# Turning k, q and y on VectorE in squares of 32, with y taken through DRAM

## The chip, the cores and the metric

One core of a Trainium2 chip. The metric is the device time of one execution in microseconds (us), the median of several executions. Executions of a kernel on one core mostly lie within 1%; each comparison below was made on one chip, in rounds that ran the two kernels alternately. An execution more than 1.5% above the fastest of its kernel is called slow; comparisons use the others.

Names: PE is TensorE (matmul), DVE is VectorE, ACT is ScalarE, POOL is GpSimd, SP is SyncE, which here issues nearly all DMAs. A line number such as L90 is that of the kernel's text; the changed kernel's numbers are shifted. The granted clock is the share of its full clock that PE was given; in these traces it is at any moment either 1 or 0.5.

## The reference

```python
q, k, v, o_gate: (4, 8, 768, 40)      # batch, heads, sequence, head dim; gates (4, 8, 768)
for t in range(S):                    # mLSTM: a decayed sum of v k^T, read with q
    C = f * C + i * outer(v[t], k[t]);  n = f * n + i * k[t]
    y[t] = sigmoid(o_gate[t]) * (C @ q[t]) / max(|n . q[t]|, 1)
x = y.transpose(0, 2, 1, 3).reshape(3072, 320)
out = ((x @ w1) * (x @ w2)) @ w3 @ w_out      # float64 weights, d_ff = 1024
```

## The kernel before

The sequence is cut into 24 units: 6 pieces of 128 tokens times 4 batches. The main loop has one step per unit and then some more. In step s, PE turns k and q of unit s (tiles pt), turns y of unit s - 3 (px), runs a product of w3 and w_out (wp, steps 10 to 17) or two output tiles (po, from step 17; step 17 has both), then the up-projections of an older group (pa, pb) and last the "cell": outputs of unit s - 1, state and scores of unit s.

```python
def turn(n):                                   # k and q, [token, head dim] -> [head dim, token]
    for src, dst, name in ((kbuf[n % NB], kT_t, "kT"), (qbuf[n % NBQ], qT_t, "qT")):
        pt = mps([128, NP, P], "pt")
        for p in range(NP):
            transpose(pt[:, p, :], src[:, 2 * p:2 * p + 2, :].rearrange("p a b -> p (a b)"))   # PE
        dst[n] = sb.tile([128, NP, P], FP, name=name, tag=name)
        nc.scalar.copy(out=dst[n], in_=pt)                                                    # ACT

def x_trans(n):                                # y -> xT, the input of the up-projections
    ...
    px = mps([128, KF + 1, P], "px")
    for cc in range(KF + 1):
        transpose(px[:, cc, :], y[:, cc * P:(cc + 1) * P])                                    # PE
    nc.scalar.copy(out=x_t[gr][:, :, j * P:(j + 1) * P], in_=px)                              # ACT
```

The weights are float64 words. DVE makes floats of them, one piece of 128 rows by 512 at a time: five operations on 128x512 and, for w3, a transpose. Up to step 15 there are one to three such conversions per step (`n_cvt`), two in each of steps 9 to 15. Before a conversion, ACT scales the raw piece.

```python
def to_f32(dst, raw):                          # L170 to L174
    V.tensor_scalar(out=t, in0=hi, scalar1=3, scalar2=None, op0=OP.logical_shift_left)
    ...                                        # three more
    V.tensor_tensor(out=dst, in0=t.bitcast(FP), in1=r.bitcast(FP), op=OP.add)

for s in range(len(n_up)):                     # the main loop, cut
    if s < NU:
        ...
        if s: turn(s)
    while turned < min(s - 2, NU):
        x_trans(turned); turned += 1
    fold()                                     # wp
    for _ in range(n_down[s]): ffn_out(*downs.pop(0))          # po
    open_ups = [up(*x) for x in now]           # pa, pb
    if len(now) < 2 and turned == s - 2 < NU:
        x_trans(turned); turned += 1
    quarter_work(s, rest)                      # ab, cell, pw, outputs
    ...
    for _ in range(n_cvt[s] if s < len(n_cvt) else 0): convert()
```

PE's instructions are pinned to the order of the program. Those of the other engines are not (after step 6): the compiler's scheduler orders each engine's instructions by its own model of readiness, and on the chip each engine runs its list in that order.

## Time and profile before

| | before |
|---|---|
| median (range) | 493.78 us (493.66 to 494.1) |
| span of the profiled run, granted clock of PE | 494.0 us, 0.98 |
| PE / DVE / ACT busy | 94% / 50% / 31% |
| stage to 146 us | PE with gaps, DVE 60 to over 90% busy |
| stage from 146 us on | PE full; a step is 16.8 us, from step 18 on 21.1 us (step 17, with wp and po, 25.4) |

"DVE 50%" is the mean of a first half in which DVE is nearly full and a second in which it is nearly idle. The slices and the step by step reading are shown in the prediction. One more line, from the view of groups of instructions by form; the columns are line, engine, operation, output and input, count, then busy us and mean ns:

```profile
L223 DVE STREAM_TRANSPOSE w3T<-w 128x512 f32<-128x512 f32 x16 | 11.3, 709 | 0.5
```

DVE's transpose of 128x512 floats took 709 ns here.

### The profile page before, as it was taken

What the parts mean: (1) busy time and instruction counts of PE and PEld (TensorE: products, weight loads), DVE (VectorE), ACT (ScalarE), POOL (GpSimd) and SP (SyncE); (2) the same over time, 40 slices, a digit from 0 to 9 for tenths busy, and PEclk for the clock granted to TensorE, in tenths of its full rate; (3) what the DMA queues carried; (4) which work ended last, traced back from release to release, by engine and by line L of the source; (5) the groups of instructions that cost most, each with busy time, mean ns of one, the idle gap of its engine ahead of it and who ended that gap; (6) DMA issues with size and microseconds to landing.
All of it is one profiled execution on the core that took longest, in us unless ns stands there. A gap on an engine that the chain in (4) does not pass through costs nothing.

```text
span 494.0 us, 13423 instructions
## 1 busy us (share of the span) xinstructions
PE 462.7 (94%) x5714; PEld 380.6 (77%) x5714; DVE 247.5 (50%) x512; ACT 153.5 (31%) x413; POOL 88.6 (18%) x163
## 2 busy tenths in 40 slices
PE   3869797899899999999999999999999998999997
PEld 2759796898677888788878787777878777777864
DVE  7787688999877978977431331403214042111110
ACT  3743454533431543354331322412112011011011
POOL 5431223621311322212410211201000000000000
PEclk9989998989999999999999999999999999999999
DMA  9999936799877737543340422311000000000001
GB/s 186 169 196 197 155 91 130 124 184 180 156 147 136 156 113 152 103 74 56 53 88 15 102 50 56 65 40 41 15 28 1 27 16 15 27 15 13 1 15 40
DMA packets 115404, 42.33 MB, mean 86 GB/s; under 512 B 103120, under 2 KB 106384, under 8 KB 115344
## 3 DMA queue, kind: packets, MB, share of 16 engines
q1 hardware_dynamic: 115200, 41.37, 41.9%
q8 instruction: 45, 0.74, 0.7%
q14 instruction: 15, 0.12, 0.1%
q10 hardware_dynamic: 144, 0.10, 0.1%
HBM read 37.42 MB, written 4.03 MB: 84 GB/s over the span
## 4 chain that ended last, share of the span: by engine, by line
PE 75%; DVE 9%; issue 7%; DMA 3%; SPq 2%; POOL 2%; ACT 1%; DVEq 0%; POOLq 0%; ACTq 0%
PE po L90 21%; PE pa L90 20%; PE pb L90 14%; PE cell L90 7%; PE wp L90 7%; PE pt L93 3%; SPq L154 2%; DVE h L349 1%; DMA raw<-in_moe_w_dram 1%; DMA pw<-U_d 1%; PE px L93 1%; DMA kbuf<-in_k_dram 1%; PE ub L90 1%; DVE h L345 1%; DVE ma L173 1%
## 5 line engine op out<-in xcount | busy, mean ns | idle before, releaser
L514 DVE TENSOR_TENSOR ab<-pb,a_sb 128x512 f32<-128x512 f32 x48 | 33.0, 690 | 182.0 <-ACT a_sb L513 181.9
L90 PE MATMUL po<-w3o,ab 128*128 128x320 f32 x384 | 105.4, 433 | 1.3 <-DVE h L349 1.3
L90 PEld LDWEIGHTS po<-w3o,ab 128*128 128x128 f32 x384 | 72.2, 190 | 30.7 <-issue 1.5
L90 PE MATMUL pa<-xT,w 128*128 128x256 f32 (+1 forms) x448 | 93.0, 355 | 0.0
L90 PE MATMUL pb<-xT,w 128*128 128x256 f32 (+1 forms) x448 | 91.9, 351 | 0.4 <-issue 0.4
L90 PEld LDWEIGHTS pa<-xT,w 128*128 128x128 f32 x448 | 77.1, 195 | 10.7 <-ACT a_sb L513 0.8
L90 PEld LDWEIGHTS pb<-xT,w 128*128 128x128 f32 x448 | 76.3, 192 | 9.0 <-issue 0.6
L513 ACT ACTIVATE a_sb<-pa 128x512 f32<-128x512 f32 x48 | 28.6, 596 | 146.6 <-PE pb L90 146.6
L90 PE MATMUL pb<-xT,wr 64*64 64x256 f32 (+1 forms) x448 | 47.4, 351 | 0.0
L90 PE MATMUL pa<-xT,wr 64*64 64x256 f32 (+1 forms) x448 | 47.4, 351 | 0.0
L283 POOL TENSOR_TENSOR state<-state,decay 128x164 f32<-128x164 f32 x40 | 19.6, 493 | 154.2 <-PE cell L90 99.1
L264 POOL TENSOR_SCALAR_AFFINE_SELECT pw<-pw 64x512 f32<-64x512 f32 x48 | 36.9, 769 | 47.1 <-ACT pw L262 44.6
L262 ACT ACTIVATE pw<-pw,aT 128x64 f32<-128x64 f32 x160 | 40.6, 339 | 5.3 <-DMA pw<-U_d 5.3
L90 PEld LDWEIGHTS pa<-xT,wr 64*64 64x64 f32 x448 | 28.5, 133 | 14.9 <-issue 6.6
L90 PE MATMUL wp<-wo,w3T 128*128 128x320 f32 x128 | 35.9, 433 | 2.0 <-DVE w3T L223 2.0
L521 ACT COPY o_sb<-po 128x320 f32<-128x320 f32 x24 | 10.2, 426 | 74.8 <-PE po L90 74.7
L90 PEld LDWEIGHTS wp<-wo,w3T 128*128 128x128 f32 x128 | 23.7, 190 | 11.1 <-issue 2.2
L90 PEld LDWEIGHTS cell<-vbuf,pw 64*64 64x64 f32 x768 | 28.2, 145 | 2.8 <-issue 0.3
L90 PEld LDWEIGHTS pb<-xT,wr 64*64 64x64 f32 x448 | 28.5, 133 | 0.0
L90 PE MATMUL cell<-vbuf,pw 64*64 64x41 f32 x768 | 28.4, 235 | 0.0
L365 POOL COPY y<-y 128x64 f32<-128x64 f32 x24 | 7.3, 306 | 110.0 <-DVE y L361 109.8
L324 DVE TENSOR_TENSOR pw<-cell,pw 128x512 f32<-128x512 f32 x24 | 16.4, 685 | 19.0 <-PE cell L90 15.4
(89 smaller groups left out, 524.4 us busy)
## 6 DMA issues: line engine op xcount, KB each, us to landing
raw<-in_moe_w_dram SPq DMA_DIRECT2D x64, 128.0 KB, 3.5
pw<-U_d SPq DMA_DIRECT2D x40, 128.0 KB, 3.7
kbuf<-in_k_dram SPq DMA_DIRECT2D x24, 160.0 KB, 4.6
qbuf<-in_q_dram SPq DMA_DIRECT2D x24, 160.0 KB, 4.9
vbuf<-in_v_dram SPq DMA_DIRECT2D x24, 160.0 KB, 4.9
o_in<-in_o_gate_dram SPq DMA_DIRECT2D x24, 160.0 KB, 4.1
out_dram<-o_sb SPq DMA_DIRECT2D x24, 160.0 KB, 1.8
raw<-in_moe_w_dram SPq DMA_DIRECT2D x7, 512.0 KB, 5.8
```

What stands on the lines that cost most here:

```text
L90: in_order(nc.tensor.matmul(out, lhsT=lhsT, rhs=rhs, start=start, stop=stop))
L93: in_order(nc.tensor.transpose(out, in_, ident[0:n, 0:n]))
L154: nc.sync.dma_start(out=dst, in_=src)
L173: V.scalar_tensor_tensor(out=r.bitcast(FP), in0=lo, scalar=2.0 ** -52, in1=r.bitcast(FP), op0=OP.mult, op1=OP.mult)
L262: nc.scalar.activation(out=pw[:, h, :], in_=src[:, h, :], func=AF.Exp, bias=aT[:, c, b * H + h:b * H + h + 1])
L264: nc.gpsimd.affine_select(out=pw[r], in_=pw[r], compare_op=OP.is_ge, fill=0.0, base=0, pattern=[[0, H], [1, L]], channel_multiplier=-1)
L283: nc.gpsimd.tensor_tensor(out=new, in0=old, op=OP.mult, in1=decay[:, b * NP:(b + 1) * NP, 2 * c + x:2 * c + x + 1] .to_broadcast([P, NP, D1]))
L324: first_read = nc.vector.tensor_tensor(out=pv, in0=ss, in1=pv, op=OP.mult)
L365: nc.gpsimd.tensor_copy(out=y_t[n][:, DM:DM + REM], in_=y_t[n][:, KF * P:DM])
L513: nc.scalar.mul(out=a_sb, in_=pa, mul=UP ** -2)
L514: nc.vector.tensor_tensor(out=ab_t[gr][j][:, fs[0]:fs[-1] + 1, t0:t0 + a_sb.shape[-1]], in0=pb, in1=a_sb, op=OP.mult)
L521: nc.scalar.copy(out=o_sb, in_=po)
```

## The change

The intent: take transposes away from PE, the bound, and give them to DVE, which is half idle. DVE's transpose is used here in squares of 32x32 (the prediction says why), so the data must come to it with the squares already in their places. k and q from unit 12 on (the 13th) are loaded from DRAM in such an order (`load_turned`, into what was the gates' space), k a second time, q only so. y from unit 8 on (the 9th) is written to DRAM in pieces (`send`) and read back rearranged (`get_back`). Separately, the first y's transposes on PE are put behind the cell of the third unit, where before they stood ahead of it and PE waited for them. Two smaller edits are cut from the diff below: the cell's matmuls that read kT and qT sum over 40 rows in place of 64, which changed nothing in the length of a full cell (2.50 us in step 11 before and 2.49 after), and the output tile has two buffers in place of three.

```diff
+    N_DVE = 12
+    NY = 8
+    def load_turned(n):                       # 8 DMAs: k and q, four neighbouring tokens to each of 32 partitions
+        ...
     def turn(n):
+        if n >= N_DVE:
+            for src, dst, name in zip(turned_in, (kT_t, qT_t), ("kT", "qT")):
+                dst[n] = sb.tile([128, NP, P], FP, name=name, tag=name)
+                nc.vector.transpose(out=dst[n].rearrange("i p (r f) -> i p f r", f=4),
+                                    in_=src[:, 32:TB].rearrange("i (p f d) -> i p f d", p=NP, f=4)[:, :, :, 0:32])
+            return
+    def send(n): ...                          # 4 DMAs, y -> y_d[n]
+    def get_back(n):
+        back_t[n] = sb.tile([P, 4, KC, 32], FP, name="yb", tag="yb", bufs=1)
+        ...                                   # 4 DMAs, y_d[n] -> yb
+    def x_turn(n):
+        nc.vector.transpose(out=x_t[gr][:, :, j * P:(j + 1) * P].rearrange("c k (m r) -> c k m r", r=32),
+                            in_=back_t.pop(n).rearrange("r m k c -> r k m c"))
...
+        if N_DVE <= s + 1 < NU:
+            load_turned(s + 1)
+        if NY <= s - 3 < NU:
+            get_back(s - 3)
+        if NY <= s - 2 < NU:
+            send(s - 2)
         while turned < min(s - 2, NU):
-            x_trans(turned)
+            x_trans(turned) if turned < NY else x_turn(turned)
...
-        if len(now) < 2 and turned == s - 2 < NU:
+        if len(now) == 1 and turned == s - 2 < NU:
```

More of the change, by code (lines that the diff above doesn't have):

```diff
@@ L95 @@
     halves = [slice(0, L), slice(L, P)]
+    heads = [slice(0, D), slice(DP, DP + D)]
     quarters = ((0, 0), (1, 1), (0, 1), (1, 0))
     NB, NBQ = 4, 3
+    N_DVE = 12
     qbuf = [const.tile([P, H, DP], FP, name=f"qbuf{i}") for i in range(NBQ)]
@@ L109 @@
     U_d = dram.tile([NT, BH, L], FP, name="U_d")
+    NY = 8
+    KC = KF + 1
+    y_d = [dram.tile([P, 4, KC, 32], FP, name=f"y_d{n}") if n >= NY else None for n in range(NU)]
     o_t, u_t = {}, {}
@@ L118, in load @@
         for dst, src in ((kbuf[n % NB][:, :, 0:D], k), (qbuf[n % NBQ][:, :, 0:D], q), (vbuf[n % NB][:, :, 0:D], v)):
-            nc.sync.dma_start(out=dst, in_=rows(src, n))
+            if src is not q or n < N_DVE:
+                nc.sync.dma_start(out=dst, in_=rows(src, n))
+    def load_turned(n):
+        c, b = divmod(n, B)
+        for dst, src in zip(turned_in, (k, q)):
+            for hip in range(2):
+                of = src[b].rearrange("(p two) s d -> two p s d", two=2)[hip, :, c * P:(c + 1) * P, :]
+                for j in range(2):
+                    p0, c0 = hip * DP + j * 32, (1 - j) * 32
+                    nc.sync.dma_start(out=dst[p0:p0 + 32, c0:c0 + NP * RAW].rearrange("r (p e) -> r p e", p=NP),
+                                      in_=of.rearrange("p (r f) d -> r p (f d)", f=4))
     def load_o(n):
@@ L305, in quarter_work @@
                 for hip, x in quarters:
-                    mm(pi[halves[x], hip, p, :], qT[halves[hip], p, halves[x]], before[x][halves[hip], p, :])
+                    mm(pi[halves[x], hip, p, :], qT[heads[hip], p, halves[x]], before[x][heads[hip], p, :])
         n, first_read = s, None
@@ L321, in quarter_work @@
                 for hip, x in quarters:
-                    mm(ss[halves[x], hip, p, :], kT[halves[hip], p, halves[x]], qT[halves[hip], p, halves[x]])
+                    mm(ss[halves[x], hip, p, :], kT[heads[hip], p, halves[x]], qT[heads[hip], p, halves[x]])
             pv = pw.rearrange("p (n two) t -> p two n t", two=2)
@@ L362, in outputs, with send @@
                                 op=OP.mult)
+    def send(n):
+        y = y_t.pop(n)
+        for cc in range(KF):
+            nc.sync.dma_start(out=y_d[n][:, :, cc, :], in_=y[:, cc * P:(cc + 1) * P].rearrange("t (i c) -> t i c", c=32))
+        for i in range(0, 4, 2):
+            nc.sync.dma_start(out=y_d[n][:, i:i + 2, KF, :], in_=y[:, KF * P:DM].rearrange("t (i c) -> t i c", c=32))
+    back_t = {}
+    def get_back(n):
+        back_t[n] = sb.tile([P, 4, KC, 32], FP, name="yb", tag="yb", bufs=1)
+        for i in range(4):
+            nc.sync.dma_start(out=back_t[n][32 * i:32 * (i + 1)].rearrange("r m k c -> r m (k c)"),
+                              in_=y_d[n][:, i].rearrange("(m r) k c -> r m (k c)", r=32))
+    def x_turn(n):
+        gr, j = divmod(n, GT)
+        if j == 0:
+            x_t[gr] = ffn.tile([128, KC, TG], FP, name="xT", tag="xT")
+        nc.vector.transpose(out=x_t[gr][:, :, j * P:(j + 1) * P].rearrange("c k (m r) -> c k m r", r=32),
+                            in_=back_t.pop(n).rearrange("r m k c -> r k m c"))
     def twice(n):
@@ L380 @@
     RG = GR * BH
-    f_sb, a, F, U, on = (const.tile([RG, TC], FP, name=n) for n in ("f_sb", "a", "F", "U", "on"))
+    RAW = 4 * D
+    TB = 32 + NP * RAW
+    gates = const.tile([P, 2 * TB], FP, name="gates")
+    f_sb, a, F, U, on = (gates[0:RG, i * TC:(i + 1) * TC] for i in range(5))
+    turned_in = [gates[:, i * TB:(i + 1) * TB] for i in range(2)]
     w, g = f_sb, on
@@ L416 @@
         nc.gpsimd.memset(t[0], 0.0)
+    nc.gpsimd.memset(gates[:, 5 * TC:2 * TB], 0.0)
+    nc.gpsimd.memset(gates[RG:P, NP * RAW:TB], 0.0)
     nc.gpsimd.memset(pick, 0.0)
@@ L519, in ffn_out @@
             mm(po, ab_t[gr][j // 2][:, f, j % 2 * P:(j % 2 + 1) * P], w3o[:, f, :], start=(f == 0), stop=(f == FO - 1))
-        o_sb = ffn.tile([P, DM], FP, name="o_sb", tag="o_sb", bufs=3)
+        o_sb = ffn.tile([P, DM], FP, name="o_sb", tag="o_sb", bufs=2)
         nc.scalar.copy(out=o_sb, in_=po)
@@ L553 @@
                 turn(s)
-        if 0 <= s - 2 < NU:
+        if N_DVE <= s + 1 < NU:
[4 more added lines that the diff above has]
+            send(s - 2)
+        elif 0 <= s - 2 < NY:
             twice(s - 2)
         while turned < min(s - 2, NU):
-            x_trans(turned)
+            x_trans(turned) if turned < NY else x_turn(turned)
             turned += 1
```

## The prediction

> **What bounds the kernel now.** I read the page first (busy shares and slices), then the chain of waits that ends last, then the timelines of VectorE (DVE) and of the DMA queue (SP). A "step" is one pass of the main loop; step s works on unit s.
>
> The slices, 12.35 us each:
>
> ```profile
> PE   3869797899899999999999999999999998999997
> DVE  7787688999877978977431331403214042111110
> PEclk9989998989999999999999999999999999999999
> ```
>
> PE is full from slice 11 on (about 146 us); before that it has gaps while DVE stands at 7 to 9 tenths. From 160 to 250 us DVE is nearly full too. The chain agrees: from 146 us to the end it is almost pure PE. Step 12 in it (start, duration):
>
> ```profile
> 162.99 1.02 PE pt L93 x8
> 164.01 0.33 PE px L93 x3
> 164.34 4.31 PE wp L90 x16
> 168.65 1.73 PE pa L90 x8
> ...
> 177.44 2.32 PE cell L90 x123
> 179.76 1.02 PE pt L93 x8
> ```
>
> So a step of this stage is pt 1.02 + px 0.33 + wp 4.31 + four pa/pb of 1.73 + 1.89 of remainder + cell 2.32 = 16.78 us, back to back. From step 17 on po (8.62) stands where wp stood: 21.08 us. Everything that leaves PE here leaves the end time, if nothing else takes its place. What DVE does in step 13:
>
> ```profile
> 180.89 0.65 DVE L324 TENSOR_TENSOR pw<-cell,pw 128x512 f32<-128x512 f32 x1
> ...
> 186.55 0.42 DVE L170 TENSOR_SCALAR ex<-raw 128x512 uint32<-128x512 uint32 x1
> ...
> 190.28 0.39 DVE L170 TENSOR_SCALAR ex<-raw 128x512 uint32<-128x512 uint32 x1
> ...
> 194.03 0.69 DVE L514 TENSOR_TENSOR ab<-pb,a_sb 128x512 f32<-128x512 f32 x1 [0.72 <-ACT a_sb L513]
> ...
> 196.61 0.69 DVE L324 TENSOR_TENSOR pw<-cell,pw 128x512 f32<-128x512 f32 x1 [0.69 <-PE cell L90]
> ```
>
> Between two pw lines (one step) DVE waits only 1.38 us for GpSimd, 0.72 and 0.69: it is nearly a second bound. It already starts pw at 180.89, 1.13 us after the cell ended at 179.76. The outputs after pw take about 4.9 us without that long GpSimd wait (165.62 to 170.49 one step earlier), one conversion of a weight piece 190.28 - 186.55 = 3.73 us, and there are two per step up to step 15.
>
> The early stage matters for the last part of the change. The timeline of PE there, and the windows of granted clock (us; busy and count of PE, PEld, DVE, ACT, POOL; clock; DMA share; GB/s):
>
> ```profile
> 33.80 0.88 PE L93 MATMUL px<-ident,y 128*128 128x128 f32 x3 [4.06 <-DVE y L361]
> ```
>
> ```profile
> 36.00:38.00 2.00, 2.00 (x78) 2.00 (x78) 0.63 (x1) 0.00 (x0) 0.00 (x0) 0.50 0.95 297
> ```
>
> PE waits 4.06 us for the first y, and afterwards the clock is half.
>
> **What the Trainium skill says.** "VectorE: DVE Perf Modes", section "The three transpose paths", says that VectorE transposes 32x32 blocks only and writes SBUF, while TensorE does 128x128 and writes PSUM. The trace agrees in kind: pt and px each need a copy by ScalarE (590 and 490 ns), while the w3T transposes on DVE write SBUF in 709 ns for 128x512. The blocks are why y must be rearranged through DRAM. "TensorE: Matmul & The Clock Gate", section "What's actually happening", says the clock falls to half after an idle window of about 3.4 us and comes back after a busy one. The trace agrees: half clock for 3.4 us after idles of 2.27 and 3.31 us, 6.8 us around the 4.06 us one. "DMA: Bandwidth & Descriptors", section "Two DMAs through the same engine are not ordered", says that a DMA that reads what another wrote must wait for its completion; get_back therefore waits for send to land. No run yet shows the length of that.
>
> **The change, part by part.**
>
> Removed from PE: pt in steps 12 to 23, 12 x 1.02 = 12.2 us; px of units 8 to 23, 16 x 0.34 = 5.4 us. All lies in the PE-bound stage: -17.6 us. The ScalarE copies that go (24 of 590 ns, 16 of 490) were beside the path.
>
> Added to DVE: two transposes of 128x512 per unit, 0.65 each back to back (kT, qT; the w3T row), and one of 128x384, about 0.55 (an estimate: 0.71 less 128 elements at the slope between the 512 and 320 element rows of L174, 0.95 ns each). So 1.9 us a step, 12 x 1.3 + 16 x 0.55 = 24.4 us in all. In steps 16 and later, where DVE has 5 to 9 us of 17 to 21, this is free. In steps 12 to 15 it isn't, and the order of the built kernel makes it worse, because DVE runs in its program's order:
>
> - Step 12: kT and qT of unit 12 stand behind the second ab of that step and a whole conversion, and the score matmuls of the same step need them. From the end of the pa/pb remainder: ScalarE copy 0.6 + ab 0.65 + conversion 3.73 + kT, qT 1.35 = 6.3 us; PE would be at the scores after 1.75. PE waits about 4.6.
> - Step 13: xT of unit 9 stands behind pw and outputs of step 12, both conversions, kT and qT of unit 13. From the end of the cell: 4.9 + 0.55 (xT of unit 8) + 2 x 3.73 + 1.35 + 0.55 = 14.8 us. PE needs it for pa after only wp, 4.3. PE waits about 10.5.
> - Step 14: units 8 and 9 are there; no wait.
> - Step 15: the same for xT of unit 11: 4.9 + 7.46 + 1.35 + 0.55 = 14.25 against 4.3. PE waits about 10.
> - Steps 16 and later: no conversions left in front, xT of unit 13 follows about 7 us after the cell and is needed after wp and po, 12.9. No wait; later xT have most of a step to spare.
>
> Sum of waits: +25 us. After each the clock should fall to half for some time. About 2.2 us lost per long wait, an estimate from the windows at 33 us (5.4 us of work at half clock, 2.7 lost) and near 80 and 101 us (3.4, 1.7 lost); twice 2.2, and 0.6 behind the first wait, where wp falls into the next wait anyway: +5 us.
>
> DMA: per late step 16 more small transfers. On SP one issue takes 0.36 to 0.6 us; a step with weights goes from 14 to 29 transfers, about 13.8 us of issuing, under the step's 15.4. Tight, but the long waits stretch these steps to over 20 us. Without weights it is about 11 of 19.7. I count 0.
>
> First y: step 2 no longer waits for it. The cell can start when the outputs have read their PSUM, 31.1 instead of 34.6, and at full clock. DVE's conversion then holds pw until 36.6 instead of 39.2: 2.6 gained there, about 3 one step later. From 61 to 129 us DVE has only short waits, so the gain should survive: -3.5 us, where up to 6 is possible if the 2.1 us of PE "issue" idle at 57.5 goes too.
>
> Sum: 493.8 - 17.6 + 25 + 5 - 3.5 = 502.7, say 503.
>
> **The rivals.** (a) The transposes fit into DVE's gaps and PE keeps its savings: 493.8 - 17.6 - 3.5 = 473 us. For it: DVE is 50% busy over the span, and the transposes of most units fall where it is a quarter busy. Against it: 1.38 + 0.72 + 0.69 us of gaps in step 13, and the order above. (b) DVE binds only by its amount, not its order: in steps 12 to 15 it would need about 13.5 + 1.9 = 15.4 us, as long as the shortened PE step, costing perhaps 3 us: 476. It would need DVE to do x before the conversions, and the built order has it after. (c) The DMA queue becomes the bound: if issues take 0.6 us or more each, or many wait for one another, 29 transfers cost over 17 us, and the back transfers delay x in every step. For it: between 30 and 60 us issues took about 1 us each, with DMA full. Against it: DMA share is 0.3 to 0.7 after 160 us. It would add 1 to 3 us to each of a dozen steps: 510 to 520.
>
> **Range and chances.** The order is read from the built program and the durations from the trace, so I trust waits of 20 to 30 us. The clock (2 to 8) and the early gain (2 to 6) move the sum by some 4 each way, and transfers can only add: 495 to 511. 2% slower is 503.7, nearly my middle. Chances: faster 0.07 (only if the order argument fails), same 0.48, slower 0.45.
>
> **What would show it.** Right: PE waits for DVE transposes of about 5, 10 and 10 us in steps 12, 13 and 15, between 170 and 260 us, half clock after them, then steps of about 19.7 us without waits; in the early stage no 4 us wait before px. Wrong: no such waits and a time near 475 (rival a or b), or PE waiting for xT behind get_back's landing in steps after 17 (rival c). The step I trust least is the early gain, and next the clock's price.

## The result, and the profile after

The changed kernel took 517.61 us (514.94 to 520.27, 4 runs), the kernel before 493.94 us (493.66 to 495.92) in the same rounds: a ratio of 1.047, 95% interval 1.041 to 1.053, so slower. Ratios here are the mean time of one kernel's fast runs over that of the other's fast runs of the same rounds, so not quite the ratio of the medians. The profiled execution had a span of 513.2 us and was the quickest of the four; the others had no trace.

The page of the changed kernel: busy time (us, share, instructions), and the slices of 12.8 us.

```profile
PE 452.4 (88%) x5570; PEld 368.7 (72%) x5570; DVE 280.3 (55%) x552; ACT 133.9 (26%) x373; POOL 83.4 (16%) x149
...
PE   3769788699899861994699999999999999999997
...
DVE  7786798999788879378565152451551431310110
...
PEclk9978899899999966998799999999999999999999
```

PE does less than before and still ends later: it falls to 6 and 1 tenths in slices 15 and 16 and to 4 and 6 in slices 19 and 20 (counted from 1), where it had been full. In these slices the clock is 6 to 8 tenths. From slice 21 on nothing is amiss.

PE's waits, in us, times, longest (the view of waits):

```profile
PE pa L90 <- DVE xT L409: 23.0, 2, 11.5
...
PE cell L90 <- DVE qT L289: 6.4, 1, 6.4
```

And where they are (timeline of PE: start, duration, operation, and in brackets the idle time before it and what ended it):

```profile
184.28 1.14 PE L90 MATMUL cell<-qT,kT 40*64 40x64 f32 x32 [6.39 <-DVE qT L289]
185.34 6.76 PE L90 MATMUL wp<-wo,w3T 128*128 128x320 f32 x16
203.59 3.58 PE L90 MATMUL pa<-xT,w 128*128 128x256 f32 x8 [11.49 <-DVE xT L409]
...
248.18 3.47 PE L90 MATMUL pa<-xT,w 128*128 128x256 f32 x8 [11.50 <-DVE xT L409]
```

The scores of step 12 wait 6.39 us, the first pa of steps 13 and 15 wait 11.5 us each: 29.4 us. After each of them the work is slow: wp takes 6.76 us instead of the 4.57 it took at full clock in step 15, pa 3.5 instead of 1.9. What DVE did before xT was ready at 203.45 (timeline of DVE, step 13):

```profile
190.37 0.49 DVE L385 TENSOR_TENSOR y<-h,o_in 128x320 f32<-128x320 f32 x1
193.15 0.43 DVE L186 TENSOR_SCALAR ex<-raw 128x512 uint32<-128x512 uint32 x1 [2.29 <-DMA y_d<-y]
...
196.89 0.85 DVE L186 TENSOR_SCALAR ex<-raw 128x512 uint32<-128x512 uint32 x1
...
201.12 1.04 DVE L289 STREAM_TRANSPOSE kT<-gates 128x512 f32<-128x512 f32 x1
202.00 1.05 DVE L289 STREAM_TRANSPOSE qT<-gates 128x512 f32<-128x512 f32 x1
202.91 0.54 DVE L409 STREAM_TRANSPOSE xT<-yb 128x384 f32<-128x384 f32 x1
```

Two whole conversions, from 193.15 to 201.12, and kT and qT of unit 13, which nobody needs before the end of the step, stand ahead of xT, which PE is waiting for. The idle time at 193.15 is put down to a DMA, but its name is not the whole story: the timeline of ACT shows the scaling of that weight piece only at 192.47, right behind the copy of wp at 192.14, and wp was the one that ran at half clock. ACT's order held up DVE, and DVE's order PE. The two lines of ACT:

```profile
192.14 0.44 ACT L255 ACTIVATE w3o<-wp 128x320 f32<-128x320 f32 x1 [12.61 <-PE wp L90]
192.47 1.20 ACT L175 ACTIVATE raw<-raw 128x512 f32<-128x512 f32 x2
```

Nor did xT wait for its data. The last load of y of unit 9 was issued at 189.6 and none of the four took over 2.3 us to land, so y was there by 191.9, before PE fell idle at 192.10; xT began at 202.91. In step 15 it was there by 236.5 (issued by 233.4, at most 3.1 to land), PE fell idle at 236.7, and xT began at 247.49.

The granted clock is the column behind the engines' busy times in the view of windows (PE, PEld, DVE, ACT, POOL busy and counts, clock, DMA share, GB/s):

```profile
179.60:189.90 10.30, 5.62 (x41) 3.94 (x42) 8.18 (x16) 0.00 (x0) 2.56 (x4) 0.50 0.28 71
196.80:207.00 10.20, 3.41 (x8) 2.79 (x9) 9.21 (x15) 0.67 (x1) 0.66 (x1) 0.51 0.95 176
241.10:251.30 10.20, 3.12 (x8) 2.55 (x9) 9.79 (x16) 2.21 (x7) 0.86 (x2) 0.50 0.65 112
```

PE worked 5.62, 3.41 and 3.12 us in these; half of it, 6.1 us, is what the clock cost (an estimate that takes the same work to need half the time at full clock).

The late steps give back a little each: in the chain, po follows the cell directly and takes 8.81 us here, where it took 8.62 behind pt and px. So a late step went from 21.07 to 19.92 us, 1.155 saved.

**The account of the two profiled spans.** Ends of the cell of each step, after against before: step 10 +0.8, step 11 -0.2 (the first px gone), step 12 +5.7, step 13 +20.0, step 14 +18.9, step 15 +31.0, step 16 +29.8, then -1.155 a step to +21.7 at step 23, and +19.2 at the end. From step 11 to 16 that is +30.05; worked out: waits 29.4, clock 6.1, five first weight loads that nothing hides any more 5 x 0.19 = 0.95, less five steps' pt and px 5 x 1.36 = 6.8, makes 29.65.

### The profile page after: what moved, and what is told of

Same layout as the page of the kernel before. It is cut to its first block, busy times and chain, and to the rows that moved or that the text cites. A ratio compares the mean times of both kernels' runs of the same rounds, so it can differ in the third digit from the quotient of the medians.

```text
span 513.2 us, 13437 instructions
## 1 busy us (share of the span) xinstructions
PE 452.4 (88%) x5570; PEld 368.7 (72%) x5570; DVE 280.3 (55%) x552; ACT 133.9 (26%) x373; POOL 83.4 (16%) x149
## 4 chain that ended last, share of the span: by engine, by line
PE 60%; DVE 13%; issue 11%; DMA 7%; SPq 4%; POOL 3%; ACT 1%; DVEq 0%; POOLq 0%; ACTq 0%
PE po L90 21%; PE pa L90 17%; PE pb L90 11%; PE cell L90 6%; PE wp L90 4%; DMA o_in<-in_o_gate_dram 2%; DMA pw<-U_d 2%; SPq L170 2%; DVE h L373 2%; DVE ma L189 1%; POOL state L307 1%; DVE ma L188 1%; DMA raw<-in_moe_w_dram 1%; DMA kbuf<-in_k_dram 1%; DVE ex L187 1%
## 5 line engine op out<-in xcount | busy, mean ns | idle before, releaser
L90 PE MATMUL pa<-xT,w 128*128 128x256 f32 (+1 forms) x448 | 98.4, 370 | 23.6 <-DVE xT L409 23.0
L90 PEld LDWEIGHTS pa<-xT,w 128*128 128x128 f32 x448 | 81.2, 207 | 36.1 <-issue 23.9
L90 PE MATMUL wp<-wo,w3T 128*128 128x320 f32 x128 | 38.7, 457 | 2.0 <-DVE w3T L239 2.0
L90 PEld LDWEIGHTS wp<-wo,w3T 128*128 128x128 f32 x128 | 24.9, 200 | 12.4 <-issue 3.8
L409 DVE STREAM_TRANSPOSE xT<-yb 128x384 f32<-128x384 f32 x16 | 9.0, 565 | 41.1 <-DMA yb<-y_d 41.1
L90 PEld LDWEIGHTS cell<-vbuf,pw 64*64 64x64 f32 x768 | 26.0, 135 | 4.0 <-issue 1.8
L90 PE MATMUL cell<-vbuf,pw 64*64 64x41 f32 x768 | 26.0, 225 | 1.4 <-issue 1.4
L90 PE MATMUL cell<-qT,kT 40*64 40x64 f32 x768 | 19.6, 237 | 8.0 <-DVE qT L289 6.4
```

The lines of the kernel that those rows point to most:

```text
L90: in_order(nc.tensor.matmul(out, lhsT=lhsT, rhs=rhs, start=start, stop=stop))
L409: nc.vector.transpose(out=x_t[gr][:, :, j * P:(j + 1) * P].rearrange("c k (m r) -> c k m r", r=32), in_=back_t.pop(n).rearrange("r m k c - ...
```

## The experiments

Twelve kernels ran. Times are medians in us; each batch's own runs of the kernel before are beside it. One of kqonly's four executions was slow: it is in the median and not in the ratio.

| run | what it is | time | before | ratio (95%) |
|---|---|---|---|---|
| late | k, q from 16, y from 12 | 485.22 | 496.58 | 0.978 (0.973 to 0.982) |
| yonly | only y, from 8 | 514.39 | 496.58 | 1.038 (1.034 to 1.042) |
| kqonly | only k and q, from 12 | 499.2 | 496.58 | 1.004 (0.999 to 1.010) |
| first | only the first y's place | 494.38 | 496.58 | 0.997 (0.991 to 1.004) |
| first5 | the same, five rounds | 495.13 | 496.74 | 0.996 (0.992 to 1.000) |
| pinned | DVE pinned to program order | 520.86 | 496.74 | 1.050 (1.046 to 1.053) |
| pin16 | pinned, k and q from 16 | 500.7 | 496.74 | 1.008 (1.004 to 1.012) |
| pincontig | pinned, contiguous kT and qT, wrong result | 519.34 | 496.74 | 1.046 (1.042 to 1.050) |
| freed | conversions behind the transposes | 491.61 | 495.06 | 0.990 (0.985 to 0.996) |
| freeddeep | freed, three buffers for yb | 489.78 | 495.06 | 0.988 (0.983 to 0.993) |
| pindeep | pinned, three buffers for yb | 520.85 | 495.06 | 1.051 (1.046 to 1.057) |
| yfree | as freed, y from 8, k and q from 16 | 493.37 | 495.62 | 0.996 (0.991 to 1.000) |

Theory A: DVE's order makes the waits; transposes that PE needs soon stand behind conversions it needs later. Rival B: DVE has too much work in steps 12 to 15, whatever the order. Rival C: the added DMAs and the round trip through DRAM are what costs.

### late: begin after the conversions

```diff
-    N_DVE = 12
-    NY = 8
+    N_DVE = 16
+    NY = 12
```

> The same two changes, begun later: k and q turned by VectorE from unit 16, y from unit 12, so that no transpose on VectorE is issued while it still converts weights. Theory A (the transposes queue behind conversions on VectorE's order in steps 12, 13 and 15, and the clock falls after each wait): the three waits of TensorE on kT and xT (29.4 us) and the half-clock stretches after 179 us are gone; eight steps keep 1.16 us each and the end some 2.5 us: about 482 us, faster than both. Theory B (VectorE has too much work whatever the order): waits of TensorE on xT or pw spread over steps 16 to 24 and the time stays above 494 us. Theory C (the extra DMA issues on SyncE are the bound): about 500 us or more, with TensorE waiting on tiles whose loads landed late.

485.22 us, faster than the changed kernel, and 1.8 to 2.7% faster than the kernel before. The window over the whole stage in which the changed kernel had its waits shows PE busy in every microsecond, at full clock (columns as above):

```profile
160.00:250.00 90.00, 90.00 (x1255) 73.49 (x1254) 68.79 (x135) 34.59 (x96) 21.54 (x33) 1.00 0.56 114
```

From step 15 to step 23 it gains 9.25 us, 1.156 a step, and 2.4 more to the end of the span. It ran 3 us above its expected 482; the kernel before, too, was 2.6 us slower in these rounds than in the first ones. DVE waited 41.8 us for y to come back in this run and PE never waited for it, so C is not what bound the changed kernel from step 16 on. A and B are not told apart by this run, since it moves the work as well as its order.

### yonly and kqonly: half the change each

```diff
-    N_DVE = 12
+    N_DVE = 24          # yonly: k and q stay on PE
```
```diff
-    NY = 8
+    NY = 24             # kqonly: y stays on PE
```

> Only y by VectorE and through DRAM (from unit 8, as in the change); k and q stay on TensorE. Theory A: the wait of step 12 on kT/qT is gone; at steps 13 and 15 xT still stands behind conversions but no longer behind kT and qT (2.2 us), so the waits at pa are about 6 to 9 us each with the half clock after them, against 11.5 each; sixteen units save 0.34 us of px each: about 494 to 505 us. Theory B (amount of work on VectorE): two thirds of the added work is gone, so nearly all waits go: about 487 us. Theory C (the round trip through DRAM and its issues is what costs): the whole 29 us of waits stays: about 517 us or more.

> Only k and q by VectorE from unit 12; y stays on TensorE. Theory A: kT and qT now stand right behind ab and before pw, conversions in front of ab; the scores wait for them some 1 to 2 us in each of steps 12 to 15 (kT and qT take 1.10 us each), perhaps with a slower clock after; no wait on xT. Gain 12 times some 0.8 us, loss 4 to 12 us: 485 to 497 us. Theory B: 24 us less of work on VectorE would still leave waits at steps 12 to 15 of about half those of the change: about 503 us. Theory C: no DRAM round trip, so no waits at all: about 483 us.

yonly was slower than A had said (494 to 505), and its waits were larger (6 to 9 expected):

```profile
PE pa L90 <- DVE xT L409: 18.7, 2, 11.9
```

I had subtracted kT and qT from the wait; but pw itself now stood behind a conversion (it began 2.4 us after the cell), the next two conversions took 8.6 us, and xT of unit 9 ended 17.1 us after the cell. So y alone, with a quarter of the added DVE work (16 x 0.565 = 9.0 us of 35.3), brings nearly the whole loss. That speaks against B: less work left the waits where they were. It agrees with C's figure too, but the trace splits the wait of step 13: PE fell idle at 186.95, y of unit 9 had landed by 192.7, and xT began at 198.21. About half of that wait is y's way through DRAM and half DVE's order.

In kqonly, kT and qT stand right behind ab, and every step from 12 to 15 has its short wait: 4.27, 1.50, 1.50 and 1.49 us, 8.8 in all. Each later step saves 0.87 us. The time, 499.2, is 2 us above the range; its profile is used for the waits only.

### first and first5: the other part of the change

```diff
-        if len(now) < 2 and turned == s - 2 < NU:
+        if len(now) == 1 and turned == s - 2 < NU:
```

> The kernel before with only the other part of the change: first y's transposes behind the third unit instead of before its up-projection. What the prediction said: 3.5 us gained, 490.3 us. What the traces say: step 2 ends 2.4 us earlier, but the clock falls all the same and the next steps wait for conversions that end when they did before: 0 (-1 to +1), 493 to 495 us.

> The kernel of the run named first once more, with more rounds, to settle the early term. Prediction: 3.5 us gained. What the first look showed: a gain of up to 2.9 us in an execution whose clock was not halved after unit 2, none where it was. Expected on the mean: 0 to 2 us gained, 0.996 to 1.0 of before.

On the mean 1.3 and 2.0 us gained, not told from nothing in three rounds and just told in five. The two profiles show why it scatters. Both end step 2 early; then PE, idle for 1.4 and 2 to 3 us, meets step 3's pa either at full or at half clock. The first line is from first, the second from first5 (timelines of PE):

```profile
38.29 2.05 PE L90 MATMUL pa<-xT,w 128*128 128x128 f32 x16 [0.84 <-ACT xT L375]
```
```profile
38.44 3.78 PE L90 MATMUL pa<-xT,w 128*128 128x128 f32 x16 [0.66 <-ACT xT L375]
```

In the first case 4.1 us are in hand after step 4 (0.9 of them from the start), in the second 0.4. The changed kernel's own trace has 3.54 us there: nothing gained.

### pinned, pincontig and pin16: the program's order on DVE

```diff
+    # before step 17: every DVE instruction traced since step 11 is made to follow the one traced before it
+    for ins in traced()[pin_from:]:
+        if ins.engine == nc.vector.engine:
+            if prev is not None:
+                tc.add_manual_dep(ins, prev.name, <order only>)
+            prev = ins
```
pin16 is the same with `N_DVE = 16`; pincontig writes `"i p (f r) -> i p f r"` in place of `"i p (r f) -> i p f r"`, so that kT and qT are contiguous and the result is wrong.

> The changed kernel with the very same work and the same units on VectorE (k and q from 12, y from 8); only VectorE's order is pinned to the order of the program from step 11 to step 16, so that in each step kT, qT and xT stand after the two conversions of the step before and ahead of ab and pw. Theory A (the order makes the waits): the 11.5 us waits at pa in steps 13 and 15 and the 6.4 us wait in step 12 are gone. VectorE's own work in such a step sums to some 16.2 us (5.0 pw to y, 7.5 conversions, 2.0 kT and qT, 0.5 xT, 1.3 ab) against 15.6 us of TensorE, so a wait of 0.5 to 1 us a step may stay at the scores: steps 12 to 15 take about what they took before, the eight later ones keep 1.16 us each and the end 2.5 us: about 480 to 484 us. Theory B (the amount of work on VectorE binds): the waits only move, and the time stays at 505 us or more.

> Wrong on purpose: as pinned, but kT and qT are written with neighbouring elements next to each other (the tokens of a unit come out in another order), to measure what the write in steps of four elements costs. Expected: kT and qT take about 0.71 us each like w3T of the same size, against 1.05 to 1.10; VectorE's work in steps 12 to 15 falls by 0.7 us a step; where pinned still waits at the scores, the wait falls by as much: 0 to 2 us less than pinned. If the strided write is not the cause, kT and qT stay at 1.05 us.

> As pinned, but k and q only from unit 16; y from unit 8 as in the change. Theory A: with y alone in steps 12 to 15 VectorE's work is about 14 us of the step's 16.4, so nothing waits at all, against 514 us for y from unit 8 without the pinned order; four more units than in the run begun late save 0.34 us of px each: about 1 us less than that run, 482 to 485 us. Theory C (the round trip of y through DRAM is too slow at steps 13 and 15): the waits at pa stay near 10 us and the time near 505 us.

All three missed. With the same work in another order, pinned took 520.86 us, as B had it. But the trace does not show DVE full. The first line is from the waits of PE, the second from the timeline of DVE, both of pinned:

```profile
PE cell L90 <- DVE qT L289: 28.6, 5, 8.4
```
```profile
193.89 0.58 DVE L409 STREAM_TRANSPOSE xT<-yb 128x384 f32<-128x384 f32 x1 [6.61 <-DMA yb<-y_d]
```

DVE stood idle for 6.6 to 7.4 us a step in steps 13 and 14, with ab, pw and the conversions behind an xT whose y had not come back. SP's queue explains the delay: the load of y comes after the eight DMAs that fetch turned k and q of the next unit (186.40 to 190.05), and those can't start before qT of this step has been read; then it takes 1.85 us to issue and some 2 to land. So the experiment did not separate order from amount: I had replaced one bad order by another. pin16 shows the same with y alone: there wp waits for w3T, 5.6 and 3.0 us in the pinned steps, as the conversions are late.

pincontig did answer its question. kT (view of groups by form) from the changed kernel, then from pincontig:

```profile
L289 DVE STREAM_TRANSPOSE kT<-gates 128x512 f32<-128x512 f32 x12 | 13.1, 1091 | 12.3 <-DMA gates<-in_k_dram 12.2
```
```profile
L289 DVE STREAM_TRANSPOSE kT<-gates 128x512 f32<-128x512 f32 x12 | 8.3, 690 | 3.9 <-DMA gates<-in_k_dram 3.8
```

The same transpose takes 1091 ns when its output goes in steps of four elements and 690 ns when it is contiguous.

### freed: only the conversions moved

```diff
+    AFTER = {12: ("qT12", "xT9"), 13: ("qT13",), 14: ("qT14", "xT11"), 15: ("qT15",)}
     # in to_f32, for a conversion traced in step s: its first operation follows those in DVE's order
+    for key in AFTER.get(step, ()):
+        tc.add_manual_dep(begun.ins, marks[key].ins.name, <order only>)
```

> The changed kernel with the same work and units; the conversions of steps 12 to 15 may not be put on VectorE ahead of qT of their own step, nor those of steps 12 and 14 ahead of xT 9 and xT 11. Nothing else is pinned. Theory A (conversions ahead of the transposes make the waits): the 6.4 us wait of step 12 goes; xT 9 and xT 11 are then bound only by the landing of y, whose load is issued after the one buffer for it is free and lands some 4 us later, so 2 to 7 us remain at pa of steps 13 and 15 in place of 11.5: 490 to 502 us. Theory B (amount of work on VectorE): the waits move to later scores or ab, 510 us or more. Theory D, formed from the run pinned (the loop of buffers: the one buffer for y coming back and the one for turned k and q, behind other issues on SyncE's queue, makes transposes late whatever the order): waits for xT at pa near 7 us or waits for qT in every step, 500 us or more.

491.61 us against the 517.61 of the changed kernel, with the same instructions on every engine. In the two traces the order of PE (pinned in both), ACT and SP is the same too; POOL's differs by one operation that changed places with its neighbour, and DVE's only in steps 12 to 15. The waits of PE that are left:

```profile
PE pa L90 <- DVE xT L417: 6.2, 2, 4.5
...
PE cell L90 <- DVE qT L297: 1.5, 1, 1.5
```

29.4 us became 7.7. And DVE in the place corresponding to the one shown above (start of step 13):

```profile
185.57 0.49 DVE L393 TENSOR_TENSOR y<-h,o_in 128x320 f32<-128x320 f32 x1
185.98 1.08 DVE L297 STREAM_TRANSPOSE kT<-gates 128x512 f32<-128x512 f32 x1
186.91 1.07 DVE L297 STREAM_TRANSPOSE qT<-gates 128x512 f32<-128x512 f32 x1
187.81 0.56 DVE L417 STREAM_TRANSPOSE xT<-yb 128x384 f32<-128x384 f32 x1
188.28 0.39 DVE L186 TENSOR_SCALAR ex<-raw 128x512 uint32<-128x512 uint32 x1
```

xT is done 2.3 us after y instead of 12.6 us, and the conversions follow. This is the run that shows theory A, and that rules out B and C for the bulk of the loss: nothing was taken off DVE, and y still went through DRAM.

### freeddeep and pindeep: more buffers for y

```diff
-        back_t[n] = sb.tile([P, 4, KC, 32], FP, name="yb", tag="yb", bufs=1)
+        if n > NY:      # q's three buffers are free once k and q come in turned
+            back_t[n] = <view of qbuf[n % NBQ]>
+        else: ...
-        if N_DVE <= s + 1 < NU: load_turned(s + 1)     # moved behind get_back and send
```

> As freed, and y coming back lands in q's three buffers, which are not used after unit 11, in place of one buffer; and its load is issued ahead of the load of turned k and q. Theory D: most of what was left in freed goes; 483 to 492 us. Theory B: no change against freed.

> As pinned (VectorE's order that of the program in steps 11 to 16), with the three buffers for y coming back and its load issued ahead of that of turned k and q. Theory D: VectorE's idle time of 6.6 to 7.4 us before xT in each of steps 12 to 16 goes, and with it the waits for qT (28.6 us): VectorE's 15.7 us of work a step then fit nearly into the step, and the time is 481 to 488 us. Theory B: waits for qT of 4 us or more a step stay, 505 us or more.

freeddeep: 489.78, and the waits for xT fall from 6.2 to 1.2 us; the waits for qT rise from 1.5 to 4.9. The gain of about 1 us over freed is inside the intervals. So what was left in freed was mostly the one buffer or the place of its load in SP's list (this run changed both), and its removal is worth little.

pindeep missed by over 30 us. DVE's wait for y fell to 3.0 to 3.6 us a step, but another of 6.0 to 7.1 us appeared behind pw, for the state on POOL. Its timelines chain up: that state stood behind POOL's masking of pw at 196.53, the masking behind ACT's pw at 194.44, and this behind ACT's copy of wp at 193.55, for which PE was late because it had waited 7.84 us for qT. As I read it, a DVE held to one fixed order passes each delay round the ring of engines; no run tests this by itself. Theory D, as I had put it (that the buffer explains pinned), fell; I made no run that separates its remaining parts.

### yfree: the order alone, for y

```diff
-    N_DVE = 12
-    AFTER = {12: ("qT12", "xT9"), 13: ("qT13",), 14: ("qT14", "xT11"), 15: ("qT15",)}
+    N_DVE = 16
+    AFTER = {12: ("xT9",), 14: ("xT11",)}
```

> y from unit 8 as in the change, k and q from 16 only, one buffer for y coming back; the conversions of steps 12 and 14 may not stand on VectorE ahead of xT 9 and xT 11. Steps 8 to 15 are those of the run yonly but for this order, so it shows what the order alone does to y. Theory A: the waits at pa of steps 13 and 15 (11.9 and 6.8 us in yonly) fall to what the one buffer leaves: xT 9 is ordered right behind xT 8, whose reading frees the buffer, so issue and landing, some 4 us after it, leave 2 to 4 us of waiting in each. The late steps as in the run late: 484 to 490 us. If the round trip as such is the cause, the waits stay at 7 us or more and the time is 497 us or more.

493.37 us, 3 us above the range. Against yonly, the waits at pa:

```profile
PE pa L90 <- DVE xT L417: 6.0, 2, 5.7
```

18.7 us became 6.0 with y's round trip as it was, so C made at most the rest. The 5.68 us that stay in step 13 are y's way back, which began late because of the single buffer and DVE's lateness: xT of unit 8 ended at 186.1, as outputs had waited 2.5 us for POOL; the load of y 9 was issued from 186.18 on, and xT of unit 9 began at 189.47.

## Why the prediction was wrong

It said 503.0, range 495 to 511; the time was 517.6. The mechanism, and the three steps it named, were right. What failed is the size of three terms of the sum: the waits, the early gain and, by little, the clock. Against the profiled span (+19.2 us where the sum says +8.9):

- **"-17.6 us" removed from PE: right in sum, in part by luck.** Step 11 gave 1.0, steps 12 to 16 5.9 (6.8 less 0.95), steps 17 to 23 8.1 and the end 2.5: 17.5 in all. Its make-up was off. A late step saves 1.155 us and not 1.36, since po's or wp's first weight load was hidden behind the transposes and no longer is. Two idle times of PE that it did not count made up for it: one of 1.15 us before pt in step 11 was 0.54 after, and one of 1.29 us before po near the end (419.69 before) was gone.
- **"Sum of waits: +25 us": 29.4.** Step 12 took 6.4 (said 4.6), step 13 11.5 (10.5), step 15 11.5 (10). The steps that failed are the durations on DVE ahead of each transpose. "kT, qT 1.35", taken from the w3T row, was 1.8 to 1.9 us, because their output is strided, which pincontig shows. "Conversion 3.73" was 3.98 in steps 13 and 15, and 4.94 in step 12, where the same operations took up to 1.02 us in place of 0.69 while POOL was at work beside them (177.53 to 181.08); why is not shown. And it had no wait of DVE for a weight piece. In step 13 two errors nearly cancelled. DVE needed 18.2 us and not 14.8: besides kT and qT, it waited 2.29 us for a weight piece behind the slow wp and the conversions took 7.97 instead of 7.46. But PE needed xT only after 6.7 us and not after 4.3, as that wp ran at half clock. In step 15, 16.0 us and not 14.25.
- **"+5 us" for the clock: 6.1**, near enough; 2.8 of it came after the first wait, where it had put 0.6, taking wp's loss to vanish in the wait that follows. It did not vanish, as DVE's next weight piece stood behind the same wp. It also called the trace in agreement with a fall after an idle window of 3.4 us, though one of its idles was 2.27 us; shorter ones follow below.
- **"First y: -3.5 us": nothing in this trace (+0.8 at step 10).** The failed step is "at full clock": step 2 did end 2.4 us earlier, but PE still has two short idles there (1.44 and 1.62 us), the clock fell all the same, and step 3 gave it back. In the two runs of that part alone, ten executions, it is worth 1.3 and 2.0 us on the mean.
- These differences add up to 4.4 + 1.1 + 4.3 + 0.1 = 9.9 of the 10.3 us that the span is off. The medians differ by 23.7 us: the profiled execution of the changed kernel was 2.7 us quicker than its median, that of the kernel before 1.7 us slower (495.68). No trace says what the other executions did.

Of its rivals, (a) and (b) supposed a DVE order which the built kernel does not have; freed comes near it, and took 491.6, not 473 to 476: most of the transposes fit, but 7.7 us of waits stay, and the -3.5 is missing there too. (c), the DMA queue as the bound, did not show in any late step, although the DMA share rose from 42% to 51% and its time range would have held the result. A right number is no evidence for a mechanism.

Range: "transfers can only add" and "the clock and the early gain move the sum by some 4 each way" allowed for each error alone; all of them went the same way.

Whether a short wait costs clock as well is not a matter of its length alone: in freed, after a wait of 1.71 us (188.51) pa ran at full clock, 1.97 us, and after one of 1.53 us (179.91) wp took 6.26 us instead of 4.5.

"DMA: Bandwidth & Descriptors" of the Trainium skill, section "Anatomy of one DMA — SWDGE (gpsimd) path", says that a wait on a semaphore happens on the issuing sequencer before dispatch. The runs agree for SP: eight loads of raw weights took 12.04 us of its queue in pindeep (193.97 to 206.01), 8.4 of them a wait for DVE, where four without a wait take 1.8 us, and what stood behind them was issued only then. This is why a load's place in the list of SP counts as much as a transpose's place in that of DVE.

## What to carry to other kernels

An engine with spare time over the whole span may have none in the stage where it is asked; read the order of its list in that stage, and ask of each new instruction what stands ahead of it that is needed later. Begin moving work where that engine falls idle: here the change begun four units later beat both kernels by doing less of it. When a scheduler orders the list, six order constraints on the late-needed work recovered about 26 us, while pinning the whole list to the program's order recovered nothing.

## What the Trainium skill lacked or had wrong

- "VectorE: DVE Perf Modes", section "The three transpose paths", gives one time for a DVE transpose (bf16, 128x128) and nothing on the layout of its output; what other pages say of steps in memory has no time for a transpose. Here, for 128x512 floats, 690 ns into contiguous memory and 1091 ns into steps of four elements.
- "TensorE: Matmul & The Clock Gate", section "What's actually happening", says of modelling that "the ramp penalty is <1% of a typical kernel span". It speaks of the warm-up at the start, so this is no contradiction but a limit: here three waits later in the kernel cost 6.1 us in clock alone, 1.2% of 513.2, and two executions of one kernel (first and first5) came apart by 2.7 us in step 3, where one ran at full and the other at half clock.
